# Fewer chunk loads placed beside the first layer's steps, more beside the second layer's products, and the hand-written tables placed anew

## The chip, the core and the metric

The kernel runs on one core of one Trainium2 chip. The metric is the device time of one execution in microseconds (us); the median of the runs shown is compared. Engines are named as in the profile: PE (matmuls), DVE, ACT and POOL (element-wise work), SP (issues transfers only). ACT and POOL issue transfers as well.

## The reference

The program is a retention block (a recurrent attention with decay) followed by a two-layer block with a gate. Cut to what matters:

```
q, k, v: (4, 8, 768, 64)                      # batch, heads, positions, head size
state = gamma[h] * state + k_t (x) v_t        # for every position t
y_t   = scale * q_t @ state
x     = y as (3072, 512)                      # 4*768 tokens, 8*64 features
h     = x @ w_in                              # w_in (512, 2048)
sp    = max(h, 0) + log1p(exp(-|h|))          # softplus
out   = (h * erf(sp)) @ w_out                 # w_out (2048, 512)
```

All of it is float32.

## The kernel before

**Blocks.** The 3072 tokens are cut into 24 chunks of 128 positions (index `j`), which the retention makes one after another, and into token blocks of 256 for the two layers. The first 512 tokens go through the two layers in the plain way, in the opening. The other 2560 tokens are worked in 20 *groups*: a group is one 256-token block against one half of the 2048 hidden features. Four groups make a *macro block*, of which there are five. Both layers use a scheme with fewer products: a 4 by 2 grid of blocks is multiplied with 26 products of sums of blocks in place of 32 products. `X_SUMS` and `W_SUMS` list the sums, `STEPS` the 26 products with what each adds to the results.

**First layer.** `first_layer(g)` is a generator with 26 steps. A step is one product: two matmuls of 128x128x128 (four records in the trace, as each float32 matmul is recorded twice) at line 1338, and one to three additions of the result from PSUM into the hidden blocks (DVE at line 1352, ACT at 1359 and 1361). Four PSUM tiles hold the products, two from the pool `hp` and two from the pool `r` (`BANKS`), so a step can't begin before its tile's older result has been read. The retention's two matmul phases (`results`, lines 1091 and 1101; `begin`, lines 947 and 1044) use tiles of the same two pools, once in every group, and `begun` (lines 1059 to 1071) reads those of `begin` on DVE.

**Second layer.** `second_layer(M)` is a generator with 26 products of 128x1024 blocks with 512x128 weights (line 1520, eight records each). Its weight sums lie in DRAM (`w_out_d`), and `load_operand` (line 1412) fetches one, 256 KB, for each product into one of four slots, at most four products ahead. `LOAD_FIRST` and `LOAD_LATER` say which queue issues it: for the first 26 products some go to SP, some to ACT, some to POOL; later nearly all to ACT. I call them operand 0, operand 1 and so on. The products of a macro block run beside the next macro block's groups: some between first-layer steps, the rest behind the last step.

**Order.** Nothing is scheduled by a tool: `AT` has for each kind of group (0 to 3 for the first four groups, then a, b, c, d in turn, then w, x, y, z for the last four) a list of `(step, action)` and a list of actions that follow behind the 26 steps. `'prod'` is a product of the second layer (with a `refill` of operands ahead of it), `'proj'` some matmuls of the opening's plain second layer (`project`, line 1215), `'xs'` sums of x blocks (lines 1271 and, for a pair in one instruction, 1274; `X_PAIRS`), `'chunk'` one part of `prepared(j + 1)` (scaling and transposing the next retention chunk; lines 814 to 832), `'rest'` whatever is left of that and of the chunk loads, followed by `results` and `begin`. `PRE` is the same for the time between the opening and group 0.

**Chunk loads.** `late_load(j)` is a generator that issues the transfers of one retention chunk: k in one transfer of 256 KB (line 408), q in 16 transfers of 16 KB (line 392), v in one (line 445), and k a second time in another layout in 16 of 16 KB (line 392). Nearly all go to SP's queue. `'begun'` makes the generator for chunk `j + 3`, and from then on it is advanced in two places, by `LD` at every `'prod'` behind the steps and by one at every first-layer step:

```
elif what == "prod":
    product()
    if ended:
        for _ in range(LD):
            next(next_load, None)
elif what == "rest":
    all_of(next_chunk)
    all_of(next_load)
```

These places fix the order of SP's queue and the order in which transfers take their semaphores. They don't delay SP by themselves: it issues its next transfer as soon as the semaphores that the transfer needs allow it.

Of the kernel before, what the change touches and what calls it, by code (L numbers as in the profile page):

```python
# [117 lines left out]
FIRST_STEPS = (('sum', 1, (0, 0), (0, 1), '-'), 0, ('sum', 0, (1, 0), (1, 1), '-'), 21, 'F', 3, 'F', 11,  # L118
# [17 lines left out]
X_ORDER = (1, 0, 2, 4, 6, 5, 12, 13, 9, 7, 14, 15, 8, 3, 17, 16, 10, 11)  # L136
# [9 lines left out]
AT = {0: ([(1, 'prod'), (1, 'chunk'), (2, 'spill'), (2, 'spill'), (6, 'in', 16), (6, 'op'), (8, 'in0', 4), (8, 'prod'),  # L146
      (8, 'proj', 1, 0, 2), (8, 'op'), (8, 'spill'), (9, 'in0', 19), (9, 'in', 15), (9, 'proj', 2, 1, 2), (9, 'prod'),
# [5 lines left out]
      (22, 'kick'), (22, 'spill'), (22, 'op'), (22, 'spill'), (22, 'chunk'), (23, 'in', 5), (23, 'spill'),  # L153
      (25, 'in', 8), (25, 'in0', 24), (25, 'op'), (26, 'in', 2), (26, 'op'), (26, 'spill'), (26, 'kick'),
      (26, 'in', 16)],
     [('rest',), ('softplus',), ('proj', 3, 1, 2), ('proj', 2, 2, 4), ('begun',), ('xs', 2), ('xs', 4), ('prod',),
      ('xs', 5), ('prod',), ('xs', 2), ('in', 30), ('prod',), ('prod',), ('xs', 11)]),
 1: ([(1, 'prod'), (1, 'in0', 27), (2, 'kick'), (2, 'in0', 30), (4, 'in', 9), (4, 'op'), (4, 'op'), (4, 'op'),
      (5, 'proj', 1, 2, 3), (5, 'kick'), (5, 'op'), (5, 'chunk'), (9, 'in', 24), (9, 'chunk'), (10, 'erf', 1),
      (12, 'kick'), (13, 'prod'), (13, 'proj', 3, 2, 3), (13, 'prod'), (14, 'in', 13), (16, 'chunk'), (18, 'kick'),  # L160
      (18, 'idle'), (19, 'kick'), (19, 'in', 3), (19, 'gate', 0, 1, 'v'), (20, 'in', 1), (20, 'proj', 3, 0, 1),
      (20, 'gate', 0, 0, 'g'), (20, 'gate', 1, 0, 'g'), (21, 'in', 30), (21, 'put', 2), (22, 'chunk'), (24, 'put', 1),
      (24, 'gate', 1, 1, 'v'), (26, 'op')],
     [('rest',), ('xs', 5), ('xs', 2), ('softplus',), ('prod',), ('prod',), ('begun',), ('prod',), ('proj', 3, 3, 4),
      ('xs', 12), ('prod',), ('xs', 4), ('xs', 1)]),
 2: ([(1, 'put', 3), (1, 'op'), (1, 'kick'), (4, 'chunk'), (6, 'kick'), (6, 'op'), (7, 'prod'), (9, 'kick'),
      (10, 'erf', 1), (11, 'gate', 0, 0, 'g'), (12, 'kick'), (13, 'gate', 1, 1, 'g'), (13, 'prod'),
      (13, 'gate', 0, 1, 'g'), (14, 'gate', 1, 0, 'g'), (15, 'chunk'), (15, 'op'), (17, 'op'), (17, 'op'), (18, 'prod'),
      (20, 'op'), (20, 'chunk'), (20, 'chunk'), (21, 'op'), (23, 'refill'), (25, 'op'), (25, 'idle'), (26, 'kick')],
     [('rest',), ('prod',), ('xs', 2), ('softplus',), ('prod',), ('xs', 14), ('xs', 5), ('xs', 1), ('prod',),  # L170
      ('begun',), ('prod',), ('xs', 2)]),
 3: ([(1, 'chunk'), (5, 'chunk'), (6, 'erf', 1), (7, 'prod'), (14, 'gate', 1, 0, 'v'), (19, 'chunk'), (19, 'idle'),
      (20, 'free'), (20, 'gate', 0, 1, 'v'), (21, 'gate', 1, 1, 'v'), (22, 'gate', 0, 0, 'v'), (24, 'new'),
      (26, 'chunk')],
     [('rest',), ('begun',), ('prod',), ('append',), ('xs', 8), ('prod',), ('softplus',), ('xs', 7), ('prod',),
      ('xs', 2), ('erf', 0), ('prod',), ('xs', 2)]),
# [3 lines left out]
       [('rest',), ('softplus',), ('xs', 7), ('refill',), ('erf', 0), ('prod',), ('xs', 3), ('xs', 8), ('begun',),  # L180
        ('xs', 1), ('prod',), ('xs', 5), ('prod',), ('prod',)]),
 'b': ([(1, 'gate', 0, None, 'g'), (1, 'gate', 1, None, 'v'), (3, 'chunk'), (4, 'next'), (5, 'chunk'), (7, 'chunk'),
        (7, 'prod'), (14, 'prod'), (16, 'chunk'), (18, 'chunk'), (19, 'kick'), (22, 'chunk'), (22, 'prod'),
        (22, 'chunk'), (25, 'kick'), (26, 'idle')],
       [('rest',), ('refill',), ('xs', 1), ('softplus',), ('erf', 0), ('begun',), ('prod',), ('xs', 5), ('prod',),
        ('xs', 2), ('xs', 7), ('prod',), ('xs', 9), ('prod',)]),
 'c': ([(1, 'gate', 1, 1, 'v'), (1, 'gate', 1, 0, 'v'), (1, 'chunk'), (5, 'chunk'), (5, 'chunk'), (8, 'next'),
# [5 lines left out]
        (8, 'gate', 0, 0, 'g'), (8, 'chunk'), (11, 'new'), (14, 'prod'), (17, 'chunk'), (19, 'chunk'), (21, 'chunk'),  # L193
        (26, 'idle')],
       [('rest',), ('refill',), ('softplus',), ('xs', 6), ('erf', 0), ('begun',), ('xs', 9), ('prod',), ('append',),
        ('prod',), ('prod',), ('xs', 3), ('prod',), ('xs', 1)]),
 'w': ([(1, 'chunk'), (1, 'gate', 0, None, 'v'), (2, 'gate', 1, 0, 'v'), (2, 'gate', 1, 1, 'v'), (3, 'prod'),
        (6, 'chunk'), (7, 'next'), (10, 'idle'), (12, 'kick'), (13, 'prod'), (14, 'chunk'), (14, 'chunk'),
        (15, 'chunk'), (19, 'chunk'), (22, 'chunk'), (23, 'kick'), (25, 'prod')],
       [('rest',), ('refill',), ('softplus',), ('prod',), ('erf', 0), ('begun',), ('prod',), ('xs', 4), ('prod',),  # L200
        ('xs', 4), ('xs', 5), ('prod',), ('xs', 6), ('xs', 5)]),
 'x': ([(1, 'chunk'), (3, 'chunk'), (5, 'next'), (6, 'gate', 0, 1, 'g'), (7, 'chunk'), (8, 'idle'), (9, 'chunk'),
        (11, 'gate', 0, 0, 'g'), (13, 'kick'), (14, 'prod'), (17, 'chunk'), (18, 'prod'), (20, 'chunk'),
        (21, 'gate', 1, None, 'g'), (23, 'prod'), (24, 'chunk')],
       [('rest',), ('xs', 3), ('refill',), ('softplus',), ('erf', 0), ('prod',), ('begun',), ('xs', 5), ('xs', 3),
        ('prod',), ('xs', 6), ('prod',), ('prod',), ('xs', 7)]),
 'y': ([(2, 'gate', 0, 0, 'v'), (4, 'gate', 1, 1, 'v'), (4, 'gate', 0, 1, 'v'), (5, 'chunk'), (5, 'gate', 1, 0, 'v'),
        (6, 'next'), (8, 'prod'), (10, 'chunk'), (10, 'chunk'), (11, 'chunk'), (13, 'prod'), (14, 'chunk'),
# [3 lines left out]
 'z': ([(1, 'gate', 0, None, 'g'), (2, 'chunk'), (3, 'gate', 1, 1, 'v'), (4, 'kick'), (4, 'gate', 1, 0, 'v'),  # L212
        (5, 'chunk'), (6, 'kick'), (7, 'prod'), (10, 'idle'), (13, 'chunk'), (14, 'chunk'), (15, 'kick'), (15, 'chunk'),
        (15, 'kick'), (17, 'new'), (20, 'chunk'), (23, 'chunk')],
# [4 lines left out]
VALUES = 'sgsvs'  # L219
# [6 lines left out]
CHUNKS = {6: 'yyyyyyyyyyyyyyyyygygygygygygygyg',  # L226
# [5 lines left out]
LOAD_ORDER = {0: 'kqvb', 11: 'kvqb', 20: 'qkvb'}  # L232

LOAD_LATER = 'sssssssssssssssssssssssssg'
LD = 3
# [9 lines left out]
EARLY = {(2, 't', 1): ['op', 'op'],  # L245
 (2, 't', 2): ['op'],
 (3, 't', 1): ['op'],
 (3, 't', 2): ['spill', 'op'],
 (3, 'u', 0): ['op', 'spill', 'spill'],
 (3, 'u', 1): ['spill'],  # L250
 (3, 'u', 3): ['op', 'spill']}
# [7 lines left out]
 'c': 'rhrh',  # L259
# [4 lines left out]
 'z': 'hrhr'}  # L264
BEGUN = {0: 'smMb',
 1: 'smbM',
 2: 'smbM',
 3: 'msMb',
 'a': 'smMb',
 'b': 'smMb',  # L270
 'c': 'smMb',
 'd': 'smMb',
 'w': 'smMb',
 'x': 'smMb',
 'y': 'smMb',
 'z': 'smMb'}
F_ORDER = {0: (0, 2, 6, 3, 1, 4, 5, 7, 9, 8, 10, 11, 13, 12, 14, 16, 15, 17, 18, 19, 21, 22, 23, 25, 24, 20),
# [44 lines left out]
def kernel(  # L322
# [1436 lines left out]
    for g in range(G0, NG):  # L1759
# [75 lines left out]
        for n, _ in enumerate(first_layer(g), start=1):  # L1835
# [61 lines left out]
```

## Time and profile before

| what | value |
|---|---|
| median of 3 runs | 655.38 us (654.84, 655.38, 659.01) |
| the profiled execution's own time | 659.89 us |
| its span | 658.2 us |
| PE busy | 645.2 us, 98% |
| DVE busy | 483.4 us, 73% |
| ACT busy | 308.2 us, 47% |
| POOL busy | 299.4 us, 45% |
| chunk transfers of 16 KB (q and k) on SP's queue | 284 and 276, landing 2.5 and 2.4 us after issue |
| operand loads on ACT's queue | 85 of 256 KB, landing 2.9 us after issue |

The opening fills the span to about 134 us, and groups 0 to 3 lie between 134 and 208 us; the first product of the second layer runs at 203 us. From 208 us on first-layer steps and products alternate; the last product begins at 652 us. PE is the engine that is always near full, so the useful reading of this profile is the list of the few places at which PE stands still, and of what it waited for there.

### The profile page before, as it was taken

The page shows a single profiled execution, that of the slowest core. Times are in us where ns is not written, and L with a number is a line of the kernel's source. Part 1 is how long each engine was busy: PE and PEld are TensorE (multiplying, and loading weights), DVE is VectorE, ACT ScalarE, POOL GpSimd, SP SyncE. Part 2 cuts the span into 40 slices and gives each one's busy share as a digit, 9 for nine tenths or more (in the row PEclk, how much of TensorE's full clock was granted, in tenths as well). Part 3 has the DMA queues.
Part 4 walks back from the last instruction along what each step waited for, and adds up shares of the span by engine and source line. Part 5 has one row for each costly group of instructions (what it writes and reads, how often), then busy time and mean ns, then how long its engine had stood idle before and what let it go on. Part 6 is the DMA issues. An engine that isn't in the chain of part 4 may idle for free.

```text
span 658.2 us, 16109 instructions
## 1 busy us (share of the span) xinstructions
PE 645.2 (98%) x6124; PEld 543.8 (83%) x6124; DVE 483.4 (73%) x1135; ACT 308.2 (47%) x525; POOL 299.4 (45%) x258
## 2 busy tenths in 40 slices
PE   8999999999999989999999999999999999999998
PEld 7744444477798879999989999999999999999887
DVE  5999888997888736867855856856866855766774
ACT  3468595417575344465453554553553652442300
POOL 1000064667667695317565237385247277255000
PEclk9999999999999989999999999999999999999999
DMA  9999887667756555455645555555555522337522
GB/s 188 228 260 252 162 246 128 107 177 191 192 127 184 109 121 121 97 115 125 135 109 126 129 117 113 135 119 130 117 110 129 124 67 74 98 95 226 192 49 48
DMA packets 221517, 91.68 MB, mean 139 GB/s; under 512 B 184768, under 2 KB 199616, under 8 KB 221440
## 3 DMA queue, kind: packets, MB, share of 16 engines
q1 hardware_dynamic: 201712, 57.79, 41.1%
q10 hardware_dynamic: 15312, 23.15, 12.5%
q0 software_dynamic: 4416, 9.71, 5.9%
q8 instruction: 48, 0.79, 0.6%
q14 instruction: 29, 0.24, 0.1%
HBM read 74.47 MB, written 13.11 MB: 133 GB/s over the span
## 4 chain that ended last, share of the span: by engine, by line
PE 82%; DVE 5%; DMA 5%; SPq 4%; issue 2%; POOL 1%; ACT 0%; ACTq 0%; DVEq 0%; POOLq 0%
PE o L1520 33%; PE hp L1338 17%; PE r L1338 13%; PE hp L1175 8%; PE o L1215 4%; SPq L392 4%; DVE w_in_sb L633 2%; DMA kb<-in_k_dram 2%; PE r L1091 1%; PE hp L947 1%; PE r L1101 1%; PE hp L1044 1%; DVE arena L1352 1%; DMA kq<-in_q_dram 1%; DMA arena<-arena 1%
## 5 line engine op out<-in xcount | busy, mean ns | idle before, releaser
L1520 PE MATMUL o<-arena 128*128 128x256 f32 x832 | 192.2, 383 | 2.4 <-DMA arena<-w_out_d 2.4
L1471 POOL TENSOR_TENSOR arena<-arena 128x1024 f32<-128x1024 f32 x75 | 176.0, 2363 | 28.9 <-PE o L1520 25.8
L1520 PEld LDWEIGHTS o<-arena 128*128 128x128 f32 x832 | 154.3, 191 | 22.4 <-issue 2.5
L1338 PE MATMUL hp<-xs,w_in_sb 128*128 128x128 f32 x816 | 118.3, 277 | 2.1 <-ACT arena L1359 1.1
L1338 PEld LDWEIGHTS hp<-xs,w_in_sb 128*128 128x128 f32 x816 | 105.8, 192 | 6.0 <-DVE arena L1352 2.0
L1352 DVE TENSOR_TENSOR arena<-arena,hp 128x256 f32<-128x256 f32 x184 | 75.2, 418 | 25.2 <-PE hp L1338 17.9
L1338 PE MATMUL r<-xs,w_in_sb 128*128 128x128 f32 x628 | 90.7, 276 | 1.2 <-ACT arena L1359 0.7
L1437 POOL COPY idle_out<-turn 128x1 f32<-128x1 f32 x52 | 15.5, 297 | 151.7 <-DVE turn L1436 151.5
L1338 PEld LDWEIGHTS r<-xs,w_in_sb 128*128 128x128 f32 x628 | 80.6, 192 | 2.8 <-ACT arena L1359 0.9
L1530 DVE TENSOR_TENSOR arena<-arena,o 128x256 f32<-128x256 f32 x89 | 36.6, 416 | 61.6 <-PE o L1520 59.3
L1352 DVE TENSOR_TENSOR arena<-arena,r 128x256 f32<-128x256 f32 x158 | 63.0, 417 | 15.1 <-PE r L1338 10.4
L1175 PE MATMUL hp<-xT,w_in_sb 128*128 128x512 f32 (+2 forms) x144 | 56.7, 548 | 0.0
L1175 PEld LDWEIGHTS hp<-xT,w_in_sb 128*128 128x128 f32 x144 | 25.7, 190 | 27.2 <-issue 24.2
L1338 PE MATMUL hp<-xT,w_in_sb 128*128 128x128 f32 x300 | 46.0, 276 | 1.7 <-issue 1.4
L1359 ACT COPY arena<-r 128x256 f32<-128x256 f32 x54 | 19.8, 374 | 52.1 <-PE r L1338 19.6
L1520 PE MATMUL o<-arena,w_in_sb 128*128 128x256 f32 x200 | 43.3, 379 | 0.0
L1338 PEld LDWEIGHTS hp<-xT,w_in_sb 128*128 128x128 f32 x300 | 40.1, 192 | 3.3 <-issue 2.2
L1520 PEld LDWEIGHTS o<-arena,w_in_sb 128*128 128x128 f32 x200 | 37.9, 190 | 5.2
L1394 POOL TENSOR_TENSOR arena<-arena,e_even 128x512 f32<-128x512 f32 (+1 forms) x22 | 36.8, 1689 | 8.5 <-ACT e_even L1385 8.4
L1110 ACT COPY xT<-r 128x256 f32<-128x256 f32 x33 | 10.8, 375 | 62.3 <-PE r L1101 62.3
L1385 ACT ACTIVATE e_even<-e_even 128x2048 f32<-128x2048 f32 x20 | 38.2, 1912 | 0.2
L741 POOL COPY idle_out<-arena 128x1 f32<-128x1 f32 x1 | 0.6, 597 | 78.6 <-ACT arena L1193 78.6
(206 smaller groups left out, 1014.1 us busy)
## 6 DMA issues: line engine op xcount, KB each, us to landing
arena<-w_out_d ACTq DMA_DIRECT2D x85, 256.0 KB, 2.9
w_in_sb<-w_out_d SPq DMA_DIRECT2D x26, 256.0 KB, 4.6
arena<-in_moe_w_out_dram SPq DMA_DIRECT2D x12, 512.0 KB, 5.4
kq<-in_k_dram SPq DMA_DIRECT2D x23, 256.0 KB, 4.3
v<-in_v_dram SPq DMA_DIRECT2D x23, 256.0 KB, 3.9
out_dram<-arena SPq DMA_DIRECT2D x152, 32.0 KB, 2.2
kq<-in_q_dram SPq DMA_DIRECT2D x284, 16.0 KB, 2.5
kb<-in_k_dram SPq DMA_DIRECT2D x276, 16.0 KB, 2.4
```

The source lines that it names most:

```text
L392: ENGINES[next(engines, "y")].dma_start(to[part, u * C : (u + 1) * C].rearrange("p (a d) -> p a d", d=32), src[2 * u + s, :, d * 32 : (d + ...
L1175: nc.tensor.matmul(HP_[ft][:, t], w_in_of(ft, kk), XC[0][:, kk, t], start=(kk == 0), stop=(kk == n_k - 1),)
L1215: nc.tensor.matmul(O[0][tt].rearrange("p (c x) -> p c x", c=4), E[g][:, u * TCH + tt * P : u * TCH + (tt + 1) * P], w_out_of(ft), start=(f ...
L1338: nc.tensor.matmul(to[:, u, :], w_in_sb[:, s, w, u * P : (u + 1) * P], x_at(x), start=first and u == 0, stop=True, skip_group_check=True,)
L1352: nc.vector.tensor_tensor(h, h, of, op=ALU.add if plus else ALU.subtract)
L1359: nc.scalar.copy(h, of)
L1385: nc.scalar.activation(e_even[:, at], e_even[:, at], AF.Erf)
L1394: engine.tensor_tensor(x, x, e_even[:, half * BL : (half + 1) * BL][:, at], op=ALU.mult)
L1437: nc.gpsimd.tensor_copy(idle_out, turn)
L1471: engine.tensor_tensor(block(blocks[to]), *ins, op=OP[sign])
L1520: nc.tensor.matmul(to, operand[:, u], rhs[:, u * 2 * P : (u + 1) * 2 * P], start=first and u == 0, stop=True, skip_group_check=True,)
L1530: nc.vector.tensor_tensor(r, r, to, op=ALU.add if plus else ALU.subtract)
```

## The change

`LOAD_PAUSES` names the eight steps 3, 6, 9, ... 24 of a group. At these the chunk-load generator isn't advanced. `LD` goes from 3 to 4: a product behind the steps advances it four times. Everything else is in the tables: actions of `AT` and `PRE` at other places, another order of a few products and sums, other PSUM pools for two kinds of group, and the choice of queue or engine for single transfers and operations.

```diff
-FIRST_STEPS = (('sum', 1, (0, 0), (0, 1), '-'), 0, ('sum', 0, (1, 0), (1, 1), '-'), 21, 'F', 3, 'F', 11,
+FIRST_STEPS = (0, ('sum', 0, (1, 0), (1, 1), '-'), ('sum', 1, (0, 0), (0, 1), '-'), 'F', 21, 3, 'F', 11,
...
  1: (during the 26 steps)
-     (5, 'proj', 1, 2, 3) ... (13, 'prod'), (13, 'proj', 3, 2, 3), (13, 'prod') ... (20, 'proj', 3, 0, 1)
+     (5, 'proj', 1, 2, 3) ... (11, 'proj', 3, 0, 1), (13, 'prod') ... (14, 'prod') ... (19, 'proj', 3, 1, 2)
     (behind them)
-     [('rest',), ('xs', 5), ('xs', 2), ('softplus',), ('prod',), ('prod',), ('begun',), ('prod',), ('proj', 3, 3, 4),
-      ('xs', 12), ('prod',), ('xs', 4), ('xs', 1)]),
+     [('rest',), ('xs', 5), ('xs', 2), ('softplus',), ('prod',), ('prod',), ('begun',), ('proj', 3, 2, 3),
+      ('proj', 3, 3, 4), ('xs', 11), ('prod',), ('prod',), ('xs', 4), ('xs', 2)]),
...
  3: (behind the 26 steps)
-     [('rest',), ('begun',), ('prod',), ('append',), ('xs', 8), ('prod',), ('softplus',), ('xs', 7), ('prod',),
-      ('xs', 2), ('erf', 0), ('prod',), ('xs', 2)]),
+     [('rest',), ('prod',), ('begun',), ('xs', 7), ('append',), ('softplus',), ('xs', 7), ('prod',), ('xs', 3),
+      ('prod',), ('xs', 2), ('erf', 0), ('prod',)]),
  'a': (behind the 26 steps)
-       [('rest',), ('softplus',), ('xs', 7), ('refill',), ('erf', 0), ('prod',), ('xs', 3), ('xs', 8), ('begun',),
+       [('rest',), ('softplus',), ('xs', 7), ('refill',), ('erf', 0), ('xs', 3), ('prod',), ('xs', 8), ('begun',),
...
-VALUES = 'sgsvs'
+VALUES = 'sssvs'
...
-CHUNKS = {6: 'yyyyyyyyyyyyyyyyygygygygygygygyg',
+CHUNKS = {6: 'yyyyyyyyyyyyyyyyygygsgygygygygyg',
...
-LOAD_ORDER = {0: 'kqvb', 11: 'kvqb', 20: 'qkvb'}
+LOAD_ORDER = {0: 'kqvb', 11: 'kvqb', 20: 'qkvb', 24: 'qkvb'}
...
-LD = 3
+LD = 4
+LOAD_PAUSES = (3, 6, 9, 12, 15, 18, 21, 24)
...
-X_PAIRS = ((1, 0), (2, 4), (17, 16))
+X_PAIRS = ((17, 16),)
...
-            next(next_load, None)
+            if n not in LOAD_PAUSES:
+                next(next_load, None)
```

In the same way, and not shown: one `'proj'` leaves `PRE` for group 0 and one leaves group 0 for group 1; the weight sums (`'in'`, `'in0'`, `'op'`), their spills to DRAM and the gate's parts stand one to a few steps earlier or later in groups 0 to 3; `F_ORDER` swaps neighbours in four kinds of group, `BEGUN` the order of four DVE operations in six, and `BANKS` the pools of two (`c`: `rhrh` to `rrhh`, `z`: `hrhr` to `hhrr`).

More of the change, by code (lines that the diff above doesn't have):

```diff
@@ L166 @@
[L166 to L171, printed above, removed]
@@ L172 @@
- 3: ([(1, 'chunk'), (5, 'chunk'), (6, 'erf', 1), (7, 'prod'), (14, 'gate', 1, 0, 'v'), (19, 'chunk'), (19, 'idle'),
-      (20, 'free'), (20, 'gate', 0, 1, 'v'), (21, 'gate', 1, 1, 'v'), (22, 'gate', 0, 0, 'v'), (24, 'new'),
-      (26, 'chunk')],
-     [('rest',), ('begun',), ('prod',), ('append',), ('xs', 8), ('prod',), ('softplus',), ('xs', 7), ('prod',),
-      ('xs', 2), ('erf', 0), ('prod',), ('xs', 2)]),
[2 rows of a table added]
+      (20, 'chunk'), (20, 'kick'), (20, 'in0', 18), (20, 'op'), (20, 'idle'), (20, 'in0', 22), (21, 'spill'),
@@ new lines @@
+ 2: ([(1, 'put', 3), (1, 'chunk'), (1, 'op'), (1, 'kick'), (4, 'prod'), (6, 'kick'), (6, 'op'), (10, 'erf', 1),
+      (10, 'kick'), (11, 'gate', 0, 0, 'g'), (12, 'kick'), (12, 'gate', 1, 1, 'g'), (14, 'gate', 0, 1, 'g'),
+      (14, 'gate', 1, 0, 'g'), (15, 'chunk'), (16, 'op'), (17, 'op'), (18, 'prod'), (19, 'op'), (20, 'op'),
+      (20, 'chunk'), (20, 'chunk'), (21, 'op'), (23, 'refill'), (25, 'op'), (25, 'idle'), (25, 'prod'), (26, 'kick')],
+     [('rest',), ('prod',), ('xs', 2), ('softplus',), ('prod',), ('xs', 14), ('xs', 5), ('xs', 1), ('xs', 2),
+      ('begun',), ('prod',), ('prod',)]),
@@ L177 @@
+ 3: ([(1, 'chunk'), (2, 'erf', 1), (5, 'chunk'), (7, 'prod'), (14, 'gate', 1, 0, 'v'), (18, 'chunk'),
+      (20, 'gate', 0, 1, 'v'), (21, 'gate', 1, 1, 'v'), (21, 'free'), (22, 'idle'), (22, 'gate', 0, 0, 'v'),
+      (24, 'new'), (25, 'chunk')],
+     [('rest',), ('prod',), ('begun',), ('xs', 7), ('append',), ('softplus',), ('xs', 7), ('prod',), ('xs', 3),
+      ('prod',), ('xs', 2), ('erf', 0), ('prod',)]),
  'a': ([(1, 'chunk'), (3, 'gate', 1, None, 'v'), (5, 'prod'), (5, 'gate', 0, None, 'v'), (6, 'next'), (9, 'chunk'),
@@ L192 @@
  'd': ([(1, 'chunk'), (2, 'kick'), (3, 'chunk'), (6, 'gate', 1, None, 'g'), (6, 'chunk'), (7, 'gate', 0, 1, 'g'),
-        (8, 'gate', 0, 0, 'g'), (8, 'chunk'), (11, 'new'), (14, 'prod'), (17, 'chunk'), (19, 'chunk'), (21, 'chunk'),
+        (8, 'gate', 0, 0, 'g'), (8, 'chunk'), (11, 'new'), (14, 'prod'), (17, 'chunk'), (18, 'chunk'), (21, 'chunk'),
         (26, 'idle')],
-       [('rest',), ('refill',), ('softplus',), ('xs', 6), ('erf', 0), ('begun',), ('xs', 9), ('prod',), ('append',),
-        ('prod',), ('prod',), ('xs', 3), ('prod',), ('xs', 1)]),
@@ L197 @@
- 'w': ([(1, 'chunk'), (1, 'gate', 0, None, 'v'), (2, 'gate', 1, 0, 'v'), (2, 'gate', 1, 1, 'v'), (3, 'prod'),
+       [('rest',), ('refill',), ('softplus',), ('xs', 8), ('erf', 0), ('begun',), ('xs', 9), ('prod',), ('append',),
+        ('prod',), ('prod',), ('xs', 1), ('prod',), ('xs', 1)]),
+ 'w': ([(1, 'chunk'), (2, 'gate', 1, 1, 'v'), (2, 'gate', 1, 0, 'g'), (3, 'prod'), (4, 'gate', 0, None, 'v'),
         (6, 'chunk'), (7, 'next'), (10, 'idle'), (12, 'kick'), (13, 'prod'), (14, 'chunk'), (14, 'chunk'),
@@ L199 @@
         (15, 'chunk'), (19, 'chunk'), (22, 'chunk'), (23, 'kick'), (25, 'prod')],
[L200 to L203, printed above, removed]
+       [('rest',), ('refill',), ('softplus',), ('prod',), ('xs', 3), ('erf', 0), ('begun',), ('prod',), ('prod',),
+        ('xs', 3), ('xs', 5), ('prod',), ('xs', 8), ('xs', 5)]),
@@ L204 @@
+ 'x': ([(1, 'chunk'), (5, 'next'), (6, 'gate', 0, 1, 'g'), (6, 'chunk'), (7, 'chunk'), (9, 'chunk'),
+        (11, 'gate', 0, 0, 'g'), (11, 'idle'), (13, 'kick'), (14, 'prod'), (18, 'prod'), (20, 'chunk'), (20, 'chunk'),
         (21, 'gate', 1, None, 'g'), (23, 'prod'), (24, 'chunk')],
[L205 to L208, printed above, removed]
+       [('rest',), ('xs', 3), ('prod',), ('refill',), ('softplus',), ('erf', 0), ('begun',), ('xs', 5), ('xs', 3),
+        ('prod',), ('xs', 4), ('prod',), ('prod',), ('xs', 9)]),
@@ L209 @@
+ 'y': ([(2, 'gate', 0, 0, 'v'), (4, 'gate', 1, 1, 'v'), (4, 'gate', 0, 1, 'v'), (5, 'gate', 1, 0, 'v'), (5, 'chunk'),
+        (6, 'next'), (8, 'prod'), (10, 'chunk'), (10, 'chunk'), (11, 'chunk'), (13, 'prod'), (15, 'chunk'),
         (19, 'chunk'), (21, 'idle'), (26, 'prod'), (26, 'chunk')],
```

84 lines of the change are left out of this document (41 added, 43 removed), and 18 rows, old and new, of tables (AT, F_ORDER, LAST_STEPS).

## The prediction

> **What bounds the kernel now.** I read the page first, then the busy time by stages, then the chain that ended last, then the waits of single places. From the page:
>
> ```profile
> PE 645.2 (98%) x6124; PEld 543.8 (83%) x6124; DVE 483.4 (73%) x1135; ACT 308.2 (47%) x525; POOL 299.4 (45%) x258
> kq<-in_q_dram SPq DMA_DIRECT2D x284, 16.0 KB, 2.5
> ```
>
> PE is the bound, and the change alters none of its matmuls. So the time can move only where PE stands still. The stages (from:to, length, busy us of PE, of its weight loads, of DVE, ACT, POOL, then granted clock) say where that is:
>
> ```profile
> 346.00:600.00 254.00, 254.00 (x2646) 237.99 (x2647) 171.70 (x466) 117.09 (x221) 127.89 (x80) 1.00 0.49 113
> ...
> 154.00:175.40 21.40, 19.79 (x244) 15.91 (x242) 15.50 (x44) 11.62 (x18) 15.18 (x19) 1.00 0.63 172
> 175.40:189.00 13.60, 13.45 (x172) 12.91 (x176) 12.09 (x38) 9.79 (x21) 7.73 (x10) 1.00 0.66 160
> 189.00:208.20 19.20, 18.28 (x316) 16.68 (x306) 15.94 (x37) 10.13 (x16) 15.04 (x15) 1.00 0.75 200
> 208.20:231.70 23.50, 22.78 (x265) 21.20 (x257) 17.82 (x49) 11.90 (x26) 14.93 (x10) 1.00 0.47 98
> 231.70:257.00 25.30, 22.94 (x142) 20.99 (x141) 12.74 (x32) 11.04 (x21) 22.13 (x12) 0.93 0.57 130
> ```
>
> The first line is the main one: from 346 to 600 us, ten groups long, PE has no idle time at all. The rest gives PE's idle time by group: 1.61 us in group 1, 0.15 in group 2, 0.92 in group 3, 0.72 in group 4, 2.36 in group 5. Elsewhere, 1.08 us lie in 340 to 348 and 0.55 at 600 to 610. Sum: 7.4 us. The largest place, as the chain and the stages have it:
>
> ```profile
> 237.11 0.66 PE hp L1338 x6
> 237.77 3.35 DMA arena<-w_out_d
> 241.12 0.14 issue
> 241.25 3.36 PE o L1520 x8
> ...
> 238.60:241.60 3.00, 0.64 (x5) 0.45 (x4) 0.77 (x2) 0.87 (x4) 3.00 (x3) 1.00 0.99 291
> 241.60:245.00 3.40, 3.40 (x11) 2.75 (x10) 0.00 (x0) 0.33 (x2) 3.40 (x2) 0.51 0.66 150
> ```
>
> PE waits for operand 9, which SP issued at 237.77 and which took 3.4 us. Then the clock is 0.51 for 3.4 us, in which the work takes 3.40 x 0.49 = 1.67 us longer. **This place costs 2.36 + 1.67 = 4.0 us.** Counting SP's issues, operand 9 stood behind all 34 transfers of chunk 12; its slot had been free since about 229.6 us, when product 5 ended. SP had issued with hardly a pause since 100 us, 0.47 us for one transfer at best (16 transfers in 7.6 us at 210 us, 16 in 10.4 us at 110 us): it is behind its program. Two other places wait for the same queue by another way. The records of the issues name a semaphore for each transfer, eight in turn, which SP and ACT share. ACT can issue an operand only when the transfer that had its semaphore before has landed, and ACT's copies out of PSUM stand behind it:
>
> ```profile
> ACT arena L1359 <- DMA kb<-in_k_dram: 4.7, 1, 4.7
> PE hp L1338 <- ACT arena L1359: 1.1, 1, 1.1
> ```
>
> That is at 345 us; 223 us is alike (0.7 us of PE).
>
> **The sum's base.** The profiled execution took 659.89 us (span 658.2 and 1.7 around it), 4.5 more than the median of 655.38, and about what the place at operand 9 costs (4.0). I take it that the median run has no such stop, and that 659.01, the slowest of the three, has one. So the forecast for the median run is worked out from 659.89 - 4.0 = 655.9, which stands 0.5 above the median; I add the terms to 655.38.
>
> **The change, part by part.**
>
> *Pauses and LD.* A chunk needs 34 advances (the first issues nothing, the second two). Before: 3 for each `prod` behind `begun`, and 26. After: 4 for each, and 18. By the table that is 38, 32, 29, 38 before for groups 0 to 3 and 34, 26, 26, 30 after; for `a`, `b`, `c`, `d` 35, 38, 38, 38 before and 30, 34, 34, 34 after. So `rest` must issue 8 at once at the end of groups 2 and 3, and 4 at the end of group 4 and of the group after each later `a`. No transfer is added or dropped. In a queue that is behind, the place in the program moves nothing by itself; it only changes who goes first, by at most about 8 x 0.47 = 3.8 us. What goes earlier: operands and spills placed in the steps (operand 8, at step 14, stands ahead of four more loads than before, 1.9 us). What goes later: an operand fetched by the third product behind `begun`, by two loads, 0.9 us (operand 5, lead 6.0 us: enough). Operand 9 comes behind `rest` in both and gains nothing. Behind the bursts `results` wants PE only, and ACT's next issue waits for a semaphore eight transfers back, as now. Cover: the leads of the operands, 4.6 us and more but for operand 9. I take 0; without the cover it costs one wait as at 345 us, 1.1 us, for each of groups 5, 9 and 13. Range -1.1 to +3.3.
>
> *A projection put into group 1's gap.* Between groups 1 and 2 PE does this:
>
> ```profile
> 172.86 1.12 PE L1215 MATMUL o<-arena 128*128 128x512 f32 x2
> 175.38 0.68 PE L1338 MATMUL hp<-xT,w_in_sb 128*128 128x128 f32 x4 [1.39 <-issue]
> ```
>
> The first step of group 2 needs PSUM that `begun` reads, and DVE comes to `begun` late, behind seven x sums. The change has a second projection there. One costs 0.87 us (32 records in 13.93 us at 54 us). The gap of 1.39 shrinks by 0.87, but DVE comes later: two pairs of sums become four single ones, which start 0.20 us apart and not 0.34, so 0.82 for 0.67. **Gain 0.87 - 0.15 = 0.7 us** (0 to 1.4), as PE's work is only moved here from places where it is full.
>
> *Values of the second group from POOL to ACT* (`VALUES`). POOL loses one of 1.04 us; ACT gains eight of 0.34, 0.24 apart, 1.9 us, six of them at `rest`, 1.45 us. ACT stands idle for 4.2 us before the copies of `results` there, so 0; without that cover `begin` waits up to 1.45 us.
>
> *One k transfer to ACT* (`CHUNKS`). SP saves 0.47 us; ACT spends as much, at a time when it is busy 5.5 of 10 us. If operand 9 is the bound, all behind it comes 0.5 earlier; in a run where it isn't, 0.
>
> *Single x sums.* 0.15 us more on DVE in each of nine other sets, hidden (DVE is busy 171.7 of 254 us where PE is full); uncovered, 1.4 us in all.
>
> *All other moves in groups 0 to 3 and later* (weight sums, spills, gates, `F_ORDER`, `BEGUN`, `BANKS`, `FIRST_STEPS`). The work is the same; only waits can go or come. Bounds: the idle time left there is 0.15 + 0.92 + 0.72, and 0.22 of group 1: 2.0 us at most to gain; a new wait of the size of group 1's, 1.4 us, to lose in each of four groups, 5.6. As most of group 1 to 3's small waits (0.2 to 0.4 us) are for DVE's and ACT's reads of PSUM, which these moves touch only by a step or two, I take -0.3. `LOAD_ORDER` 24 is never read: the last chunk is 23.
>
> **Sum:** 655.38 + 0 - 0.7 + 0 + 0 + 0 - 0.3 = **654.4 us**.
>
> **The rivals.**
>
> *R1, the other side: operand 9 stops every run.* Place: product 9 in group 5. SP's queue reaches operand 9 at its own pace, and PE reaches product 9 a microsecond earlier when the gaps ahead of it close. What is won ahead of it turns into waiting, and the stop comes with its slow clock. It decides from the point where the operand lands over some 2 us after PE is ready. Price: 655.4 + 4.0 - 0.5 (SP's saved issue) = **658.9 us**. For it: operand 9 isn't moved, one of three runs and the profile seem to have the stop already. Against it: two runs seem not to. The Trainium skill (TensorE: Matmul & The Clock Gate, Part 1) lets the clock fall only after an idle window of some 3.4 us; by that rule a stop of 2.4 us costs 2.4, and R1 would be 657.3 us. Here the slow clock followed a stop of 2.36 us, so the trace doesn't agree, and I keep 4.0.
>
> *R2: the bursts of `rest` hold ACT.* Operand loads on ACT take their semaphores right behind four loads of a backlogged SP, as at 345 us, and its PSUM copies wait: 3.3 us for groups 5, 9, 13 and one stop at operand 9: 655.4 + 3.3 + 4.0 = **662.7 us**. For it: 4.7 us of ACT lost in this way already. Against it: between 430 and 450 us ACT waits 2.7 us for a transfer in the same way, and PE loses nothing.
>
> *R3: the tables close the gaps.* All idle time but operand 9's goes: 7.4 - 2.4 = 5.0, so 650.4 (a little lower, as the matmuls' ends are modelled and hide short gaps); half of it **652.9 us**. For it: the projection sits exactly in a gap. Against it: the waits at 223 and 345 us hang on SP's backlog, which stays.
>
> *R4: it does nothing*, since a late queue doesn't follow the places of its loads: **655.4 us**.
>
> **How the numbers follow.** Forecast 0.33, R1 0.22, R2 0.12, R3 0.18, R4 0.15. I predict 654.4 us. One per cent is about what a measurement of this kernel can tell from no change: 648.8 and 661.9 are its ends. Faster by more needs 6.6 us, all idle time outside operand 9 and the hidden gaps: a quarter of R3, 0.05. Slower by more: R2 and a little of R1, 0.13. Within: 0.82. The range of 650.0 to 661.5 leaves out most of R2 and the far end of R3, under 0.2; the forecast's own is 652.5 to 656.
>
> **What would show it.** Right: two projections (four records at line 1215) before the first matmul of group 2 and a gap of about 0.65 us there; PE full from 346 to 600 us; operand 9 again issued by SP right behind the last k transfer of chunk 12. Wrong: idle PE beyond 346 us, above all in a group behind an `a` (R2); a stop at product 9 in all runs (R1), or SP reaching operand 9 more than 1 us earlier (R3).

## The result, and the profile after

| | median us | runs | lowest to highest |
|---|---|---|---|
| before | 654.86 | 20 | 653.82 to 659.01 |
| after | 656.80 | 20 | 655.74 to 659.02 |

The ratio of the runs is 1.0025, 95% interval 1.0014 to 1.0036; it is worked out from all of them, and the two medians stand a little further apart (1.9 us). By the ratio the kernel became slower by 1.6 us, a small step, but the interval doesn't reach 1; 1.0 us faster was forecast. The profiled execution of after took 657.23 us, with a span of 655.5 and the full clock throughout, against 659.89 and 658.2 before. The two profiles compare badly as wholes, since that of before held the stop at operand 9 with its slow clock. So I compare them place by place, and PE's work is the same, as the page shows:

```profile
PE 642.9 (98%) x6124; PEld 541.6 (83%) x6124; DVE 486.0 (74%) x1153; ACT 310.2 (47%) x533; POOL 299.1 (46%) x257
```

The stages of after, in the same columns as before:

```profile
154.00:177.00 23.00, 21.97 (x269) 17.31 (x258) 18.11 (x53) 15.25 (x27) 13.42 (x17) 1.00 0.63 169
203.00:210.00 7.00, 5.40 (x130) 4.88 (x133) 6.31 (x10) 0.75 (x3) 5.88 (x5) 1.00 0.63 193
232.00:257.00 25.00, 25.00 (x228) 23.38 (x218) 14.59 (x36) 12.00 (x23) 24.06 (x12) 1.00 0.51 122
346.00:600.00 254.00, 252.21 (x2636) 236.03 (x2634) 170.53 (x477) 115.78 (x218) 128.47 (x83) 1.00 0.49 113
```

There is no stop at operand 9 (PE 25.00 of 25.00), nor at 223 or 345 us. But 1.60 us are idle in the 7 us from 203 on, where before had no gap, and 1.79 in the long stage that had none: 1.24 at 416 us, and 0.55 at 598 us, which before has too, at 601 us and so just outside this stage. From here on, a gap is what a matmul's start lies late by, against the usual distance of its kind; it comes out 0.1 or 0.2 us larger than the idle time.

| gap at | before | after | what PE waits for |
|---|---|---|---|
| 110 us | - | 0.59 | a copy on ACT behind an accumulating transfer of POOL |
| 138 us | - | 0.97 | DVE's reads of `begin` (`begun`) |
| 174 us | 1.55 | 0.81 | the same, group 1 |
| 206 us | - | 1.76 | DVE's read of a first-layer product, group 3 |
| 223 us | 0.88 | - | ACT's copy behind a transfer |
| 239 us | 2.52, and 1.67 of slow clock | - | operand 9 |
| 345 us | 1.24 | - | ACT's copy behind a transfer |
| 416 us | - | 1.40 | ACT's copy behind a transfer |

The forecast gap of group 1 came out as forecast. The timeline has start, length, engine, line, operation, and in brackets the idle time ahead:

```profile
173.79 1.98 PE L1217 MATMUL o<-arena 128*128 128x512 f32 x4
176.43 0.68 PE L1340 MATMUL hp<-xT,w_in_sb 128*128 128x128 f32 x4 [0.66 <-PE o L1217]
```

(L1217 and L1340 are lines 1215 and 1338 of before.) Two projections stand ahead of the first matmul of group 2, and 0.66 us of gap are left.

The new gap at 206 us, in the waits of 203 to 209 us (who waits for whom: us, times, longest), and then in the timeline of POOL and of DVE:

```profile
PE hp L1340 <- DVE arena L1354: 1.6, 1, 1.6
```

```profile
204.50 2.34 POOL L1473 TENSOR_TENSOR arena<-arena 128x1024 f32<-128x1024 f32 x1 [0.49 <-DMA kq<-in_q_dram]
207.47 2.37 POOL L1473 TENSOR_TENSOR arena<-arena 128x1024 f32<-128x1024 f32 x1 [0.63 <-DVE arena L1396]
...
204.60 2.79 DVE L1396 TENSOR_TENSOR arena<-arena,e_even 128x512 f32<-128x512 f32 x1
207.32 0.41 DVE L1354 TENSOR_TENSOR arena<-arena,hp 128x256 f32<-128x256 f32 x1
```

DVE's last product of the gate (L1396) takes 2.79 us; its line's group has 685 ns in the median. It began 0.1 us behind the first of POOL's two sums (L1473) and ended 0.55 us behind that sum's end: it was held while POOL worked. The read of PSUM behind it (L1354) came at 207.32, and PE needed that tile. Before, both sums stood behind the gate's last product; this is the timeline of before, whose product took 0.69 us:

```profile
204.61 4.69 POOL L1471 TENSOR_TENSOR arena<-arena 128x1024 f32<-128x1024 f32 x2 [1.71 <-DMA kq<-in_q_dram]
...
203.84 0.69 DVE L1394 TENSOR_TENSOR arena<-arena,e_even 128x512 f32<-128x512 f32 x1
```

The change swaps the two sums in `FIRST_STEPS` (the same line puts sum 1 behind product 0 and an `'F'` one place ahead). Sum 0 reads blocks that are gated earlier, so POOL may start it while DVE still gates. The theory for what follows: **this swap makes the kernel slower.** Rivals: the pauses do, or another of the tables, or stops at operand 9.

### The profile page after: what moved, and what is told of

Read it like the earlier page. It is cut to its first block, busy times and chain, and to the rows that moved or that the text cites. A ratio compares the mean times of both kernels' runs of the same rounds, so it can differ in the third digit from the quotient of the medians.

```text
span 655.5 us, 16141 instructions
## 1 busy us (share of the span) xinstructions
PE 642.9 (98%) x6124; PEld 541.6 (83%) x6124; DVE 486.0 (74%) x1153; ACT 310.2 (47%) x533; POOL 299.1 (46%) x257
## 4 chain that ended last, share of the span: by engine, by line
PE 81%; SPq 6%; DVE 5%; DMA 5%; ACT 2%; issue 1%; ACTq 0%; DVEq 0%
PE o L1522 32%; PE hp L1340 17%; PE r L1340 14%; PE hp L1177 6%; SPq L394 4%; PE o L1217 3%; DMA kq<-in_q_dram 2%; PE r L1093 2%; DVE w_in_sb L635 1%; PE r L1103 1%; PE hp L1315 1%; PE hp L949 1%; PE hp L1046 1%; DVE arena L1354 1%; DMA kb<-in_k_dram 1%
## 5 line engine op out<-in xcount | busy, mean ns | idle before, releaser
L1473 POOL TENSOR_TENSOR arena<-arena 128x1024 f32<-128x1024 f32 x75 | 175.9, 2361 | 27.5 <-PE o L1522 25.0
L1340 PE MATMUL hp<-xs,w_in_sb 128*128 128x128 f32 x808 | 116.7, 276 | 2.5 <-DVE arena L1354 2.2
L1340 PEld LDWEIGHTS hp<-xs,w_in_sb 128*128 128x128 f32 x808 | 104.3, 192 | 6.2 <-DVE arena L1354 3.6
L1340 PE MATMUL r<-xs,w_in_sb 128*128 128x128 f32 x636 | 91.7, 276 | 1.8 <-ACT arena L1361 1.2
L1354 DVE TENSOR_TENSOR arena<-arena,hp 128x256 f32<-128x256 f32 x178 | 72.8, 417 | 16.7 <-PE hp L1340 12.5
L1340 PEld LDWEIGHTS r<-xs,w_in_sb 128*128 128x128 f32 x636 | 81.5, 192 | 3.4 <-ACT arena L1361 1.4
L1354 DVE TENSOR_TENSOR arena<-arena,r 128x256 f32<-128x256 f32 x164 | 65.5, 417 | 20.3 <-PE r L1340 13.7
L1340 PE MATMUL hp<-xT,w_in_sb 128*128 128x128 f32 x292 | 44.8, 276 | 1.0 <-PE o L1217 0.7
L1396 POOL TENSOR_TENSOR arena<-arena,e_even 128x512 f32<-128x512 f32 (+1 forms) x23 | 38.1, 1670 | 15.7 <-ACT e_even L1387 15.6
L1340 PEld LDWEIGHTS hp<-xT,w_in_sb 128*128 128x128 f32 x292 | 39.2, 192 | 3.1 <-issue 1.9
L1361 ACT COPY arena<-r 128x256 f32<-128x256 f32 x46 | 16.9, 373 | 44.4 <-PE r L1340 17.8
L1340 PE MATMUL r<-xT,w_in_sb 128*128 128x128 f32 x240 | 36.6, 275 | 0.0
```

Source lines behind the costliest of these rows:

```text
L1340: nc.tensor.matmul(to[:, u, :], w_in_sb[:, s, w, u * P : (u + 1) * P], x_at(x), start=first and u == 0, stop=True, skip_group_check=True,)
L1354: nc.vector.tensor_tensor(h, h, of, op=ALU.add if plus else ALU.subtract)
L1361: nc.scalar.copy(h, of)
L1396: engine.tensor_tensor(x, x, e_even[:, half * BL : (half + 1) * BL][:, at], op=ALU.mult)
L1473: engine.tensor_tensor(block(blocks[to]), *ins, op=OP[sign])
```

## The experiments

Each ran beside the kernel before on the same chip. Ratios are to before, with 95% intervals.

### Which part it is

**The kernel before, again**

> The kernel before, unchanged, profiled once more. Theory 'tables' (the slow-down of 0.25% is the sum of single gaps of PE that the moved table entries opened: 0.6 us at 110 us, 1.0 at 138, 1.6 at 206, 1.4 at 416, against 0.7, 0.9 and 1.2 us won at 173, 223 and 345): an execution without the stop at operand 9 shows the gaps at 173, 223 and 345 and a span near 654. Rival 'pauses' (the loads' new places cost the time): the gaps at 223 and 345 are absent in an undisturbed execution of before, so that the change can't have won them. Ratio 1.000 in both.

Ratio 1.0004 (0.9989 to 1.0018). Its profiled execution took 654.31 us, with a stop of only 0.99 us at operand 9 and no slow clock. That fits my assumption that the large stop belongs to the slower executions; two profiles don't show it. The gaps at 223 and 345 us are not there either, so the change can't be said to have won them. Ahead of group 2 only 0.56 us are idle, where the first profile had 1.39, but `begin` ended 0.8 us later: group 2 starts at 175.37 us in this one and at 175.38 in the other.

**The pauses and `LD` alone, on the tables of before**

```diff
-LD = 3
+LD = 4
+LOAD_PAUSES = (3, 6, 9, 12, 15, 18, 21, 24)
```

> The kernel before with only LOAD_PAUSES and LD = 4, all tables as before. Theory 'tables': the gaps at 110, 138 and 206 us are absent, since no table moved; the gaps that hang on SP's queue (223, operand 9, 345) may change by up to 1.2 us each, so between -2.1 and +1.5 us, ratio 0.997 to 1.002. Rival 'pauses': most of the loss is here, +1.6 us, ratio 1.0025, with new waits of ACT for chunk transfers in groups behind a burst of rest.

0.9992 (0.9979 to 1.0005): nothing that can be measured.

**The tables of after alone**

```diff
-LD = 4
-LOAD_PAUSES = (3, 6, 9, 12, 15, 18, 21, 24)
+LD = 3
+LOAD_PAUSES = ()
```

> The changed kernel with LOAD_PAUSES empty and LD = 3. Theory 'tables': the gaps at 110, 138 and 206 us are all there (3.2 us together), so at least 1.003, and the gap at 416 may go. Rival 'pauses': the loss is gone, ratio 1.000 or below.

1.0050 (1.0032 to 1.0068). The loss is in the tables. Its profile has the gap of 206 us (1.76) and one of 2.05 at 110 us, with a slow clock behind it (3.50 us at 0.57, shown at the end: 1.5 us) that the profile of after doesn't have. That is about the size by which 1.0050 stands above after's 1.0025; whether the pauses have a part in it, these six runs don't show.

### The swap of POOL's sums

**After, with `FIRST_STEPS` of before**

```diff
-FIRST_STEPS = (0, ('sum', 0, (1, 0), (1, 1), '-'), ('sum', 1, (0, 0), (0, 1), '-'), 'F', 21, 3, 'F', 11,
+FIRST_STEPS = (('sum', 1, (0, 0), (0, 1), '-'), 0, ('sum', 0, (1, 0), (1, 1), '-'), 21, 'F', 3, 'F', 11,
```

> The changed kernel with FIRST_STEPS of before (the sum of blocks that reads the last gated block first again). Theory 'tables': POOL's sum can't begin until DVE's gate product has ended, the gate product takes 0.7 us and not 2.8, the gap of 1.6 us at 206 goes, 1.0 to 1.6 us less than the changed kernel, ratio to before 1.000 to 1.001. Rival 'pauses': unchanged, 1.0025.

1.0007 (0.9987 to 1.0026), and the gap at 206 us is gone. POOL waits for DVE, and the product is short:

```profile
205.82 4.70 POOL L1473 TENSOR_TENSOR arena<-arena 128x1024 f32<-128x1024 f32 x2 [1.36 <-DVE arena L1396]
...
205.05 0.69 DVE L1396 TENSOR_TENSOR arena<-arena,e_even 128x512 f32<-128x512 f32 x1
```

**Before, with `FIRST_STEPS` of after** (the converse)

> The kernel before with one line of the change: FIRST_STEPS of the kernel after. The converse of the run that put FIRST_STEPS back. Theory (POOL's first sum now overlaps DVE's last product of the gate, which is held): that product takes some 2.8 us instead of 0.7, PE has a gap of 1.4 to 1.8 us at about 206 us, and the time goes up by that less what the stop at operand 9 gives back (it was 0.99 us in the repeat of before): 0.6 to 1.6 us, ratio 1.001 to 1.0025. Rival (the order of the first products matters, not POOL's overlap): no long gate product, and a gap at another place or none; ratio 1.000.

1.0029 (1.0008 to 1.0049), a loss as large as the whole change's from one line. The product takes 2.79 us beside POOL's sum, and PE's gap is 2.09 us, at 210 us in this execution:

```profile
208.31 2.34 POOL L1471 TENSOR_TENSOR arena<-arena 128x1024 f32<-128x1024 f32 x1 [2.06 <-DVE arena L1394]
...
208.40 2.79 DVE L1394 TENSOR_TENSOR arena<-arena,e_even 128x512 f32<-128x512 f32 x1
```

**After, with POOL held behind DVE.** This keeps the new order and takes away only the overlap: a column that DVE copies behind the gate's last product and POOL reads ahead of its sums.

```diff
-       (24, 'new'), (25, 'chunk')],
+       (24, 'kick'), (24, 'new'), (25, 'chunk')],
```

> The kernel after with one action more, a kick ahead of the new in group 3: a copy of one column on DVE and one on POOL that reads it, so POOL's first sum starts behind DVE's last product of the gate. The order of FIRST_STEPS stays that of after. Theory (it is the overlap that costs): the gate's product takes 0.7 us again, the gap at 206 us goes (1.76 us in after), the time falls by 1.2 to 1.7 us against after, to a ratio to before of 0.999 to 1.001. Rival (the new order itself, for instance POOL's sums coming too late for the first product): the gap stays at 206 us or moves to the first product at about 203 to 208 us, ratio 1.0025.

1.0002 (0.9986 to 1.0019): as before, and 1.5 us below after. In the same 7 us PE is full:

```profile
203.00:210.00 7.00, 7.00 (x157) 6.42 (x157) 5.74 (x17) 2.96 (x5) 5.50 (x5) 1.00 0.66 210
```

What was the order's fault is thus the overlap's. The profiles of all runs agree: this product took 2.79 to 2.81 us in the six with the new `FIRST_STEPS` and no such copy, and 0.68 or 0.69 in the fourteen others. This profile has a stop of 2.39 us at operand 9, which after's had not: PE came to product 9 2.1 us earlier, and SP issued the operand at 237.38 us, 1.75 us later than in after.

**After, again, on the chip of other runs**

> The kernel after, unchanged, beside the others on the same chip. Ratio 1.0015 to 1.0035; a gap of 1.7 us at 206 us and one of 0.8 us at 175 us in its profile. If the gap at 206 us were an accident of the one profile, it would not be there, and the ratio would be near that of the kick.

1.0026 (1.0012 to 1.0039). The gaps stand again at 138 (1.19), 175 (0.81) and 206 us (1.77), and there is none at 416.

### Theories that fell

The gaps at 110 and 138 us made me suspect other edits. One is `EARLY`, a table that the change touches too and the section on the change doesn't name (nor does it `W_IN_ORDER`, `W_IN_POOL`, `X_ORDER` and `LAST_STEPS`, which no run changed alone).

**After, with `EARLY` of before** (which weight sums stand between the opening's products)

```diff
-EARLY = {(2, 't', 1): ['op'],
+EARLY = {(2, 't', 1): ['op', 'op'],
...
```

> The changed kernel with EARLY of before (two weight sums at once after the second token block of the opening's third part, in place of one each after two blocks). Theory 'tables, EARLY': POOL's third accumulating transfer goes out earlier, ACT is held less long, the gap of 0.5 us at 110 goes, 0.4 to 0.6 us less than the changed kernel, ratio to before about 1.001 to 1.002. Rival 'only chance': such a gap has been seen with the old EARLY too (0.6 us with the pauses alone), so it stays or goes by itself, ratio 1.0025.

1.0047 (1.0029 to 1.0066), with a gap of 2.64 us at 110 us and 0.98 at 140. `EARLY` makes neither. The gap at 110 us was 0 to 2.64 us in profiles of kernels with equal work there: ACT waits 5.1 us (in after) for an accumulating transfer that POOL issues at 105 to 108 us, and PE's copy is queued behind it. What decides when POOL issues it stays open.

**After, with the projection back in `PRE`**

```diff
-(2, 'spill'), (4, 'proj', 2, 0, 1), (8, 'prod'),
+(2, 'spill'), (8, 'prod'),
...
-('in', 22), ('op',), ('in', 19), ('begun',),
+('in', 22), ('proj', 2, 0, 1), ('op',), ('in', 19), ('begun',),
```

> The changed kernel with one projection put back from group 0 into the opening's end (PRE). Theory 'tables, projection': its 0.87 us of PE work covers the wait for begun at 138 us, the gap of 0.8 to 1.0 us goes, and nothing new opens, 0.8 us less than the changed kernel, ratio to before about 1.0013. Rival 'the work is only moved': group 0 then has the idle time instead, ratio 1.0025.

1.0015 (0.9993 to 1.0036). The gap at 138 us stays, at 0.98.

**After, with all three back** (the three diffs above: `FIRST_STEPS`, `EARLY`, the projection)

> The changed kernel with FIRST_STEPS and EARLY of before and the projection put back: what is left are the pauses, the second projection in group 1's gap and the other moves. Theory 'tables': -1.6 - 0.5 - 0.9 us from the changed kernel, about 653.9, ratio 0.998. Rival 'other moves': a good part of the loss lies in moves that are still there (gates, spills, weight sums), ratio 1.000 or above.

1.0029 (1.0011 to 1.0047), with 2.25 us at 110 us and none at 138, since PE came later there. These three can't be added up term by term; the gap at 110 us varies by more than what they were to show.

The gap at 138 us is better read from after's own timeline:

```profile
132.71 5.29 DVE L635 TENSOR_TENSOR w_in_sb<-w_in_sb 128x256 f32<-128x256 f32 x1
...
138.58 0.41 DVE L1071 COPY state<-hp 128x256 f32<-128x256 f32 x1
...
139.14 1.10 PE L1315 MATMUL hp<-xT,w_in_sb 128*128 128x256 f32 x4 [0.81 <-DVE state L1071]
```

A weight sum on DVE (usually 0.42 us) is held for 5.29 us, beside three sums of POOL from 133.07 to 137.7. It looks like the same holding, and before had it as well (timeline of DVE in before, and the group of its line):

```profile
131.62 0.74 DVE L1059 TENSOR_TENSOR am<-hp,causal_d 128x256 f32<-128x256 f32 x2
...
133.07 6.08 DVE L633 TENSOR_TENSOR w_in_sb<-w_in_sb 128x256 f32<-128x256 f32 x3
```

```profile
L633 DVE TENSOR_TENSOR w_in_sb<-w_in_sb x51: 411/420/5409, 110.6 to 157.9; 128x256 f32<-128x256 f32 x51
```

But in before DVE made `begun`'s reads (from 131.62) ahead of the held sum (from 133.07), and in after behind it (from 137.92), so now PE waits for them. No run changed this order alone, so this is a reading and not shown by an experiment.

### Where the gain of group 1 went

**Before, with the pauses and group 1's projection in its gap**

```diff
-       (13, 'proj', 3, 2, 3),
...
-('begun',), ('prod',), ('proj', 3, 3, 4),
+('begun',), ('proj', 3, 2, 3), ('prod',), ('proj', 3, 3, 4),
```

> The kernel before with the pauses and LD = 4, and one projection moved from step 13 of group 1 to the gap behind begun; no other table is touched. Theory 'tables': the gap between groups 1 and 2 shrinks by 0.87 us and no other opens, about 0.7 us less than the pauses alone, ratio 0.998. Rival 'the gap is given back': PE comes to a later wait (operand 9) earlier and waits there, ratio 0.999 to 1.000 as with the pauses alone.

1.0023 (0.9998 to 1.0049): no gain, though the gap at 174 us fell from 1.55 to 0.70. The profile has a stop at product 9 instead, for which SP issued the operand at 236.06:

```profile
226.37 9.58 SPq L393 DMA_DIRECT2D kb<-in_k_dram  x16
236.06 0.84 SPq L1413 DMA_DIRECT2D arena<-w_out_d  x2
...
239.40 1.32 PE L1521 MATMUL o<-arena 128*128 128x256 f32 x5 [1.93 <-DMA arena<-w_out_d]
```

**The refill ahead of `rest`**, with and without the projection's move

```diff
-       [('rest',), ('softplus',), ('xs', 7), ('refill',), ('erf', 0),
+       [('refill',), ('rest',), ('softplus',), ('xs', 7), ('erf', 0),
```

> The kernel before with the pauses, LD of 4 and group 1's projection moved into the gap (as in the run with the pauses and the gap), and in groups of kind a the refill ahead of rest: operand 9 then stands ahead of the four chunk loads that are left over, 4 x 0.47 = 1.9 us earlier on SP's queue. Theory (what was won in group 1 was given back at operand 9): the stop at operand 9, 2.09 us in that run, falls to 0 to 0.5 us, and the time to a ratio of 0.997 to 0.999 to before. Rival (the stop hangs on the landing, or on something other than the place in the queue): the stop stays above 1 us, ratio 1.000 to 1.002.

> The kernel before with the pauses and LD of 4 alone, and in groups of kind a the refill ahead of rest. In the run of the pauses alone there was no stop at operand 9 in the profile. Theory: this takes away the stop in the executions that have one; ratio 0.997 to 0.9995, gap of 1.4 us at 174 us as in before. Rival (the stop is rare or the bursts of rest were not in the way): ratio as that of the pauses alone, 0.9992.

1.0003 (0.9982 to 1.0023) and 1.0002 (0.9983 to 1.0022). Both expectations rest on a mistake of mine: with before's tables and `LD` of 4 nothing of chunk 12 is left over at that `rest`, so operand 9 did not move on SP's queue, and the stop stayed (1.62 and 1.70 us). Both profiles also have 1.14 and 1.15 us of idle PE at 204 to 206 us, a gap that stands in no other profile with the `FIRST_STEPS` of before. There POOL's weight sum runs beside the two gate products ahead of the last, which take 2.59 and 2.60 us together instead of 1.28 (timelines of DVE and of POOL, second run):

```profile
201.85 2.60 DVE L1395 TENSOR_TENSOR arena<-arena,e_even 128x512 f32<-128x512 f32 x2
...
202.09 1.81 POOL L1612 TENSOR_TENSOR arena<-arena 128x512 f32<-128x512 f32 x1
```

So such an overlap can come without the swap, when times shift.

**The same edit on after's tables** (with the kick), where four loads are left over, and then thirteen:

```diff
-            if n not in LOAD_PAUSES:
+            if n not in LOAD_PAUSES and not (i == 4 and n > 13):
```

> The kernel after with the kick ahead of new (POOL behind DVE) and, in groups of kind a, the refill ahead of rest. With the tables of after four of chunk 12's loads are left over at rest in group 4, so operand 9 goes out ahead of the last four, some 4 x 0.47 = 1.9 us earlier. Theory (operand 9 follows its place on SP's queue and takes back what is won ahead of product 9): the stop, 2.39 us in the profile of the kick alone, falls below 0.8 us; ratio 0.998 to 0.9995. Rival (the stop is not set by SP's queue): a stop above 1.5 us stays; ratio 1.000 to 1.001.

> As the run with four loads behind operand 9, and in group 4 the chunk loads aren't advanced behind step 13, so that thirteen of the sixteen last loads of chunk 12 come behind operand 9, some 13 x 0.5 = 6 us earlier. Theory: operand 9 is issued at 229 to 232 us, soon after its slot is free, there is no stop, the next operand (10, behind those thirteen loads, lead 4 us and more) may be the next to be late; ratio 0.997 to 0.9995. Rival: the wait only moves, to operand 10 or to the copies of results, and the ratio is 1.000 to 1.002.

0.9995 (0.9978 to 1.0012) and 1.0006 (0.9990 to 1.0022). SP reached operand 9 at 231.1 and 230.4 us, 7 and 8 us ahead of its product, and neither has a stop for it. Against the kick alone (1.0002) the time does not tell them apart: with thirteen there is a new gap of 0.70 us at 241 us, and the one at 138 us stays in both (1.04 and 1.09).

**The gap of group 1 and operand 9 ahead of twelve loads** (the run with the gap, the refill ahead, and `n > 8` in the line above)

> The kernel before with the pauses, LD of 4, group 1's projection moved into the gap, the refill ahead of rest, and in group 4 no chunk load advanced behind step 8, so that twelve of chunk 12's last loads come behind operand 9. This is the test that the run with the refill alone was meant to be. Theory: the 0.7 to 0.85 us won at 174 us is kept, there is no stop at operand 9; ratio 0.997 to 0.999. Rival (something else than operand 9 takes it back): ratio 1.000 to 1.002, with a new stop between 240 and 346 us that is larger than in before.

0.9986 (0.9964 to 1.0008). As its interval still touched the others, it was run a second time, side by side with the kernel that has the gap's move alone:

> The kernel of the pauses and the gap, again: before with the pauses, LD of 4 and group 1's projection in the gap; operand 9 behind all of chunk 12's loads. Theory (operand 9 takes the gain back): ratio 1.000 to 1.002, with a stop of 1.5 us and more at operand 9 in the profile. Rival (it does not): a ratio like that of the run beside it.

> The same with operand 9 ahead of twelve of chunk 12's loads, again. Theory: no stop at operand 9, ratio 0.9975 to 0.9995, and 0.0015 or more below the run beside it. Rival: within 0.001 of the run beside it, and then it does not matter where operand 9 stands.

1.0013 (0.9998 to 1.0027) without operand 9's move, **0.9981 (0.9968 to 0.9993)** with it, 2.1 us apart by these ratios. The profiled execution without the move is the fastest of its twelve (653.58 us), with a stop of only 0.34 us of idle time, where more than 1.5 was expected: SP reached the operand at 234.08. With the move the operand goes out in time (timeline of SP) and PE is full (stages):

```profile
228.40 0.45 SPq L1413 DMA_DIRECT2D arena<-w_out_d  x1
228.91 6.90 SPq L393 DMA_DIRECT2D kb<-in_k_dram  x12
```

```profile
236.00:240.00 4.00, 4.00 (x31) 3.79 (x30) 2.09 (x4) 1.51 (x5) 3.90 (x3) 1.00 1.01 280
```

So in this kernel the time is won once operand 9 is moved. How much of the gain is the projection's is not shown, as no run moved the operand in before's tables without it. With the operand behind all sixteen loads SP issued it at anything from 234.08 to 238.18 us in seven profiles of before's tables, with and without the projection's move, so the stop changes from one execution to the next. This version, at 654.29 us against 654.98, is a little faster than before, and so than after, which stands at 1.0026.

## Why the prediction was wrong

**The step that failed is the last term, "All other moves … I take -0.3".** Its sign was wrong. It argued that the small waits are for reads of PSUM which the moves touch by a step or two, and put `FIRST_STEPS` among them without asking which instructions of DVE and POOL would now run side by side. That swap alone cost 1.2 to 1.9 us by the ratios (after's 1.0025 against 1.0007 with the line undone; 1.0029 with the line alone; 1.0002 with the overlap taken away, and the line kept). The bound "a new wait of the size of group 1's, 1.4 us" was about the right size for one group: it became 1.76 us at one place. The trace of before already showed the risk: DVE's weight sum of 5.41 us at 133 us, beside POOL, where others of its kind take 0.42.

The Trainium skill (SBUF — State Buffer, Who interferes with whom) states it as a rule: "A DVE instruction with two SBUF inputs contends with a GpSimd instruction that reads SBUF" (GpSimd is POOL), and whichever comes second is held. The trace agrees: DVE's product, 0.1 us behind POOL's sum, took 2.79 us and not 0.69. I had not weighed that rule.

**The projection, -0.7, was right at its place and wrong in the sum.** The gap shrank by 0.74 us. It did not reach the end (1.0023 and 1.0013 with the move alone): the term counted a gain ahead of product 9 as a gain of the whole, while SP's queue set when product 9 could start. That is R1's mechanism, "what is won ahead of it turns into waiting", and it worked without R1's price for the clock, which was 1.00 behind the stops of 1.62 to 2.39 us in four later profiles. With the operand moved as well the kernel came to 0.9981.

**Pauses and `LD`, 0, right:** 0.9992. Operand 9 followed the sixteen k transfers as forecast (issued at 235.6 us in after, 236.4 in its repeat; 237.8 and 235.1 in the two of before). `VALUES`, `CHUNKS` and the single x sums were not run alone; after without the overlap is 1.0002, which leaves their sum, with the projection, the other moves and the gap at 138 us, within about 0.2% of nothing.

**The base:** 655.38 was 0.5 above the median of the twenty runs. The assumption that the profiled stop is no part of the median run held only in part: smaller stops of 0.5 to 2.1 us stand in five of the six profiles that were taken later of before's tables with operand 9 in its old place (three of the five with the projection moved).

**R2's wait** was seen once (4.2 us of ACT behind a k transfer at 416 us, 1.2 us of PE), and not in the repeat, where 253.45 of the 254 us from 346 on are busy and the rest is the gap at 598 us. **R3** was right in that gaps went at 223 and 345 us in the profiles of after; but those two also went in other profiles of before's tables, so the change can't be given them. **R4**, no effect, is right for the part that gives the change its name, and wrong for its tables.

## What to carry to other kernels

Before two independent element-wise streams are reordered, look up which of their instructions will run side by side: a DVE operation whose inputs both lie in SBUF, beside a POOL sum, may cost most of the POOL sum's length (2.1 of 2.34 us here), and it delays everything queued behind it. An order that seems to wait for nothing may have been what kept them apart. And a gap closed ahead of a late transfer was worth nothing here until the transfer's place in its queue was changed too; close both, or measure both together.

## What was not expected of the hardware

**Which DVE operations are held.** In after, the 265 reads of PSUM by DVE (L1354) that overlap a sum or product of two inputs on POOL by 0.1 us or more took 0.42 us at most, no longer than the 77 others; their group shows it beside the gate's products (count: shortest/median/longest ns):

```profile
L1354 DVE TENSOR_TENSOR arena<-arena,hp x178: 373/420/423, 158.5 to 605.0; 128x256 f32<-128x256 f32 x178
L1354 DVE TENSOR_TENSOR arena<-arena,r x164: 380/420/422, 161.0 to 604.1; 128x256 f32<-128x256 f32 x164
L1396 DVE TENSOR_TENSOR arena<-arena,e_even x37: 648/685/2790, 167.6 to 611.9; 128x512 f32<-128x512 f32 x25, 128x1024 f32<-128x1024 f32 x12
```

So one input in PSUM kept an operation free of it. The weight sum of 5.29 us lasted past three POOL sums in a row, not only past the first; its record starts at 132.71 us, 0.36 ahead of the first of them, so the profile doesn't settle what held it at first. And which of the two is held can differ between executions of one kernel: at 170.06 us DVE's gate product and POOL's weight sum (L1611) start within 0.01 us of each other, and took 0.69 and 1.80 us in the profile of before, 1.84 and 1.28 in its repeat.

**The slow clock isn't set by the length of a stop alone.** A stop of 2.36 us of idle PE was followed by 3.4 us at 0.51 in before, one of 1.90 us of idle time (the gap of 2.05 at 110 us) by 3.5 us at 0.57 in the run with the tables alone:

```profile
112.00:115.50 3.50, 3.23 (x4) 1.36 (x5) 3.33 (x10) 0.71 (x2) 1.92 (x3) 0.57 1.19 230
```

The run with `EARLY` of before had 2.48 us of idle time there (the gap of 2.64), and the full clock right behind it:

```profile
113.00:116.50 3.50, 3.50 (x9) 1.59 (x10) 3.33 (x10) 0.36 (x1) 1.19 (x2) 1.00 1.13 198
```

R1's price of 1.67 us for the clock is thus paid by some stops and not by others. What decides it was not tried.
